# Block-diagonal product of an attention block as two products of 288 columns in one tile of two PSUM banks

## The chip, the core and the metric

The kernel runs on one core of a Trainium2 chip. The metric is the device time of one execution in microseconds; where several runs are shown, their median. TensorE is called PE here (its weight loads PEld), VectorE DVE, ScalarE ACT, GpSimd POOL and SyncE SP, as the profile does.

## What is computed

```python
# q, k, v: batch 8, heads 8, sequence 576, head size 64; float32
kv  = einsum('bhsd,bhse->bhde', k, v)           # 64 x 64 for each head
out = einsum('bhsd,bhde->bhse', q, kv)
rms = sqrt(mean(out * out, axis=-1, keepdims=True) + 1e-06)
x   = out / rms * g_norm                        # -> (4608 tokens, 512)
h   = x @ w_in                                  # 512 -> 2048
sp  = maximum(h, 0) + log1p(exp(-abs(h)))       # softplus
y   = (h * erf(sp)) @ w_out                     # 2048 -> 512
```

## The kernel before

The tokens of one batch entry are worked on as 512 columns (`G`), and the other 64 of each (`R`) are gathered from all eight entries into a ninth step of 512 columns. So `T` counts nine steps: 0 to 7 are the entries, 8 (`B`) the gathered rests. Features lie on partitions, tokens on columns.

**The feed-forward part** fills most of PE's time. From T = 2 (`FIRST`) on, every large product is made from three FP32R products: `product()` (L449) accumulates eight in `n_ps` and four in `m_ps` (L462), and the three forms of each operand are cut by ACT and DVE (`upper`, L405; `lower`, L408 and L411). ACT (L836) and DVE (`add`, L445) join the two sums. Six PSUM banks go round for these products, so a pair of banks comes up again three products later. The hand-written order runs in batches of four blocks of 128 hidden features: four `hidden` products, then four `result` products of the batch before (L847 to L861).

**The attention of entry T + 1** is spread over the batches of entry T, one pair of heads (`p`, 0 to 3) to a batch. `attention()` returns a pair's pieces, and the loop puts them at the places 0, 2, 3, 5, 6 and 8 of a batch (L801):

- `products` (place 0): k^T v of two heads into the diagonal blocks of a bank (L297); in even pairs the transpose of q's last rows for two pairs (L305); DVE's copies of the two blocks into `bd_kv` (L312) and, in even pairs, of the transposed rests into `qT_last` (L315); four transposes of q (L319) and ACT's copy of them into `qT` (L320).
- `apply` (place 2): the product of the rest, 64 columns, into the k-v bank (L324), the product of the 512 columns (L325), DVE's copy of the former into `x_last` (L326), ACT's Square of the latter (L328).
- `halve` (place 3): DVE cuts the squares into an FP32R part and a rest (L338, L339), for T from 2 to 7 (`halves`).
- `mean` (place 5): two FP32R products with a block-diagonal matrix of 1/64 accumulate the mean square (L346, L347); ACT makes the inverse root from it by Ln, Exp and Square (L358 to L360).
- `norm` (place 6): a correction step on DVE (L366, L369) and the scaled output (L378), which reads the L325 bank for the last time.
- `split` (place 8): the three forms of the new x.

For entry 2 the same pieces are laid into the steps of T = 1 (`pieces_of`, L599), and for T = 0 and 1 the mean is one float32 product (L351). All PSUM tiles of a pair come from `ps_at`, a pool of two banks used in turn: k-v products, q's transposes, the 512-column product, the mean. So the next pair's k-v products write the bank that L378 reads last. The framework puts in the waits between engines; the order on each engine is that of the program.

In float32 a product is issued as two PE instructions, in FP32R as one.

Of the kernel before, what the change touches and what calls it, by code (L numbers as in the profile page):

```python
# [39 lines left out]
FP32 = mybir.dt.float32  # L40
# [3 lines left out]
AF = mybir.ActivationFunctionType  # L44
ALU = mybir.AluOpType
PSUM = bass.MemoryType.PSUM
# [8 lines left out]
FIRST = 2  # L55
# [5 lines left out]
def kernel(  # L61
# [10 lines left out]
    nc = tc.nc  # L72
    P = 128
    B, H, S, D = q.shape
    DM, DF = moe_w_in.shape[0], moe_w_in.shape[1] // 2
    J = 4
    G = J * P
    R = S - G
# [8 lines left out]
    attp = ctx.enter_context(tc.tile_pool(name="attp", bufs=1))  # L87
# [5 lines left out]
    first_w = room.enter_context(tc.tile_pool(name="first_w", bufs=1, side="right"))  # L93
    gate = room.enter_context(tc.tile_pool(name="gate", bufs=7, side="right"))
    early = early_room.enter_context(tc.tile_pool(name="early", bufs=2))
    ps_at = ctx.enter_context(tc.tile_pool(name="ps_at", bufs=2, space=PSUM))
    ps_h = ctx.enter_context(tc.tile_pool(name="ps_h", bufs=2, space=PSUM))
    ps_o = ctx.enter_context(tc.tile_pool(name="ps_o", bufs=1, space=PSUM))

    ctx.enter_context(tc.manual_schedule())  # L100

# [51 lines left out]
    for i in range(2):  # L153
        nc.gpsimd.dma_start(
            out=g_col[i * D : i * D + D, :], in_=g_norm.rearrange("(d one) -> d one", one=1)
# [11 lines left out]
    ident = const.tile([P, P], FP32, name="ident")  # L167
    make_identity(nc, ident)
    mean_w = const.tile([P, P], FP32R, name="mean_w")
# [13 lines left out]
    x_last = const.tile([P, KC, G], FP32, name="x_last")  # L183
# [79 lines left out]
    xT, x_forms, tails = {}, {}, {}  # L263
# [5 lines left out]
    def attention(T, p, pools=None):  # L269

        st = {}

        halves = FIRST <= T < B
        bd = bd_kv[:, (T * NP + p) % 2, :]

        q_tail, o_tail = slice(P, 2 * P), slice(2 * P, 2 * P + R)

        def bank(name):
            pool, tag = (pools or {}).get(name, (ps_at, "at"))
            return pool.tile([P, G], FP32, name=name, tag=tag)  # L280

        def square_tile(name):

            if T == 0:
                return gate.tile([P, G], FP32, name=name, tag="h")
            return attp.tile([P, G], FP32, name=name, tag="qT")

        def products():

            kv_ps = st["kv"] = bank("kv_ps")  # L290
            ks, vs, qs = (x.pop((T, p)) for x in (k_sb, v_sb, q_sb))
            C = chunks(T)
            for c in range(C):
                rows = slice(0, S // C + (c < S % C))
                for i in range(2):
                    s = slice(i * D, i * D + D)
                    nc.tensor.matmul(  # L297
                        kv_ps[s, s],
                        lhsT=ks[rows, i, c],
                        rhs=vs[rows, i, c],  # L300
                        start=(c == 0),
                        stop=(c == C - 1),
                    )
            if p % 2 == 0:
                nc.tensor.transpose(kv_ps[:, q_tail], q_last[:, p // 2], ident)  # L305
            if p == NP - 2:
                for i in range(NP):
                    load_last(T + 1, i)
            st["qT"] = square_tile("qT")
            for i in range(2):  # L310
                s = slice(i * D, i * D + D)
                nc.vector.tensor_copy(out=bd[s, s], in_=kv_ps[s, s])  # L312
            if p % 2 == 0:
                tails[T] = attp.tile([P, P], FP32, name="qT_last", tag="t")
                nc.vector.tensor_copy(out=tails[T], in_=kv_ps[:, q_tail])  # L315
            st["tail"] = tails[T][:, p % 2 * R : p % 2 * R + R]
            qt_ps = bank("qt_ps")
            for j in range(J):
                nc.tensor.transpose(qt_ps[:, j * P : j * P + P], qs[:, j], ident)  # L319
            nc.scalar.copy(st["qT"], qt_ps)  # L320

        def apply():
            qT, o_ps, kv_ps = st["qT"], bank("se_ps"), st.pop("kv")
            nc.tensor.matmul(kv_ps[:, o_tail], lhsT=bd, rhs=st.pop("tail"), start=True, stop=True)  # L324
            nc.tensor.matmul(o_ps, lhsT=bd, rhs=qT, start=True, stop=True)  # L325
            nc.vector.tensor_copy(out=x_last[:, p, T * R : T * R + R], in_=kv_ps[:, o_tail])  # L326
            st["o"] = o_ps
            nc.scalar.activation(qT, o_ps, AF.Square)  # L328

        def square():  # L330
            st["o"], st["qT"] = x_last[:, p, :], square_tile("sq")
            nc.scalar.activation(st["qT"], st["o"], AF.Square)

        def halve():
            sq = st.pop("qT")
            hi = st["hi"] = attp.tile([P, G], FP32R, name="sq_hi", tag="rms_r")
            lo = st["lo"] = attp.tile([P, G], FP32R, name="sq_lo", tag="sq_lo")
            nc.vector.tensor_copy(out=hi, in_=sq)  # L338
            nc.vector.tensor_tensor(out=lo, in0=sq, in1=hi.bitcast(FP32), op=ALU.subtract)  # L339

        def mean(table=True):
            ms = st["ms"] = bank("ms_ps")
            if halves:


                nc.tensor.matmul(ms, lhsT=mean_w, rhs=st.pop("hi"), start=True, stop=False)  # L346
                nc.tensor.matmul(ms, lhsT=mean_w, rhs=st.pop("lo"), start=False, stop=True)  # L347
                u = square_tile("u")
            else:
                u = st.pop("qT")  # L350
                nc.tensor.matmul(ms, lhsT=mean_w.bitcast(FP32), rhs=u, start=True, stop=True)  # L351
            if T > 0:
                r = attp.tile([P, G], FP32, name="rms_r", tag="rms_r")
                exp_ln_table()
            else:
                r = gate.tile([P, G], FP32, name="rms_r", tag="s")
            st["u"], st["r"] = u, r
            nc.scalar.activation(r, ms, AF.Ln, bias=eps_col)  # L358
            nc.scalar.activation(r, r, AF.Exp, scale=-0.5)
            nc.scalar.activation(u, r, AF.Square)  # L360
            if table and (T > 0 or p == NP - 1):
                softplus_table()

        def norm():
            ms, u, r = (st.pop(name) for name in ("ms", "u", "r"))
            nc.vector.scalar_tensor_tensor(  # L366
                out=u, in0=ms, scalar=EPS, in1=u, op0=ALU.add, op1=ALU.mult
            )
            nc.vector.scalar_tensor_tensor(  # L369
                out=u, in0=u, scalar=3.0, in1=r, op0=ALU.subtract, op1=ALU.mult  # L370
            )
            if T < FIRST:
                if T not in xT:
                    xT[T] = wide.tile([P, KC, G], FP32, name="xT", tag="ab"[T])
                x = xT[T][:, p, :]
            else:
                x = st["x"] = x_new.tile([P, G], FP32, name="x", tag="x")
            nc.vector.scalar_tensor_tensor(  # L378
                out=x,
                in0=st.pop("o"),  # L380
                scalar=gm_col,
                in1=u,
                op0=ALU.mult,
                op1=ALU.mult,
            )

        def split():
            if T >= FIRST:
                thirds(st.pop("x"), *(form[:, p] for form in x_forms[T]))

        def loads():
            load_pair(T * NP + p + 2)

        if T == 0:
            return products, apply, halve, mean, norm
        if T == B:
            return lambda: None, square, lambda: None, mean, norm, split

        pieces = ((products,), (apply,), (halve, loads)) if halves else ((products, loads), (apply,), ())
        return (*(partial(chain, *group) for group in pieces), mean, norm, split)  # L400


# [111 lines left out]
    o_ps = {}  # L514
# [129 lines left out]
    for n in range(FIRST * FC + 1):  # L644
        T, f = divmod(n, FC)
        if n == FC:
            early_room.close()
            late = ctx.enter_context(tc.tile_pool(name="late", bufs=1))
            x_new = ctx.enter_context(tc.tile_pool(name="x_new", bufs=1))
            acc = ctx.enter_context(tc.tile_pool(name="acc", bufs=1))  # L650
            w_in_p = ctx.enter_context(tc.tile_pool(name="w_in_p", bufs=BATCH))
            low = low_room.enter_context(tc.tile_pool(name="low", bufs=1))
            forms = late.tile([P, 3, KC, G], FP32R, name="x_forms0")
            x_forms[FIRST] = [forms[:, i] for i in range(3)]
# [24 lines left out]
        elif T < FIRST:  # L679
# [10 lines left out]
            for i, c in blocks:  # L690
                nc.tensor.matmul(  # L691
                    plain[i],
                    lhsT=w_in_sb[:, c, i % FC * P : i % FC * P + P],
                    rhs=xT[T][:, c, :],
                    start=(c == 0),
                    stop=(c == KC - 1),
# [89 lines left out]
    for m in range(first_batch, batches + 1):  # L786
        T, b = divmod(m, NB)
# [108 lines left out]
```

## Time and profile before

| | us |
|---|---|
| median of 3 runs | 948.07 (947.21 to 948.4) |
| profiled execution, device time | 947.5 |
| its span in the profile | 945.7 |
| PE, PEld busy | 926.8, 683.3 |
| DVE, ACT busy | 740.5, 615.7 |
| float32 product of 512 columns, L325: 64 instructions | 35.4 |
| float32 product of 64 columns, L324: 64 instructions | 10.9 |
| FP32R products of the mean, L346 and L347: 24 each | 9.5 and 9.5 |

The profile is of one execution, and its span lies 1.8 us below that execution's device time. "Busy" is the union of an engine's instructions; the ends of PE's are modelled, and neighbouring ones overlap, so one instruction's recorded duration is not its price: the step from one end to the next is. The granted clock of PE was 1.0 throughout. The page gives for each group of instructions the line, the engine, the tiles it writes and reads, the count, the busy time, the mean duration and what ended the idle time before it.

### The profile page before, as it was taken

The page shows a single profiled execution, that of the slowest core. Times are in us where ns is not written, and L with a number is a line of the kernel's source. Part 1 is how long each engine was busy: PE and PEld are TensorE (multiplying, and loading weights), DVE is VectorE, ACT ScalarE, POOL GpSimd, SP SyncE. Part 2 cuts the span into 40 slices and gives each one's busy share as a digit, 9 for nine tenths or more (in the row PEclk, how much of TensorE's full clock was granted, in tenths as well). Part 3 has the DMA queues.
Part 4 walks back from the last instruction along what each step waited for, and adds up shares of the span by engine and source line. Part 5 has one row for each costly group of instructions (what it writes and reads, how often), then busy time and mean ns, then how long its engine had stood idle before and what let it go on. Part 6 is the DMA issues. An engine that isn't in the chain of part 4 may idle for free.

```text
span 945.7 us, 11743 instructions
## 1 busy us (share of the span) xinstructions
PE 926.8 (98%) x4272; PEld 683.3 (72%) x4272; DVE 740.5 (78%) x1054; ACT 615.7 (65%) x825; POOL 2.4 (0%) x10
## 2 busy tenths in 40 slices
PE   6999999999999999999999999999999999999998
PEld 4444445665688888888888888888888888878886
DVE  3979958888578788777788888878887877777667
ACT  3889876777666666666666666666666666665552
POOL 1000000000000000000000000000000000000000
PEclk9999999999999999999999999999999999999999
DMA  9856505899699998998899889998896778768872
GB/s 258 282 158 215 169 9 215 310 339 340 219 364 346 317 303 284 315 301 303 275 295 314 303 288 311 312 301 294 293 323 261 265 247 352 284 245 309 335 273 60
DMA packets 111842, 259.78 MB, mean 275 GB/s; under 512 B 43864, under 2 KB 69544, under 8 KB 111784
## 3 DMA queue, kind: packets, MB, share of 16 engines
q1 hardware_dynamic: 110152, 256.73, 78.4%
q10 hardware_dynamic: 1568, 2.29, 0.8%
q8 instruction: 34, 0.56, 0.2%
q14 instruction: 24, 0.20, 0.1%
q0 software_dynamic: 64, 0.00, 0.0%
HBM read 224.40 MB, written 34.60 MB: 274 GB/s over the span
## 4 chain that ended last, share of the span: by engine, by line
PE 88%; ACT 5%; DVE 5%; DMA 1%; issue 1%; DVEq 0%
PE n_ps L462 45%; PE m_ps L462 23%; PE o_ps L520 8%; PE h_ps L691 3%; PE se_ps L325 3%; PE kv_ps L297 2%; PE qt_ps L319 2%; ACT w_e L215 1%; ACT w_m L219 1%; DMA q_sb<-in_q_dram 1%; PE ms_ps L347 1%; PE ms_ps L346 1%; PE ms_ps L351 1%; ACT L103 1%; ACT s_sb L719 1%
## 5 line engine op out<-in xcount | busy, mean ns | idle before, releaser
L462 PE MATMUL n_ps<-x_forms,w_in_parts 128*128 128x512 f32 x896 | 233.2, 402 | 1.6 <-DVE x_forms L408 0.7
L462 PE MATMUL n_ps<-w_out_parts,g_forms 128*128 128x512 f32 x928 | 231.2, 391 | 0.0
L462 PEld LDWEIGHTS n_ps<-w_out_parts,g_forms 128*128 128x128 f32 x928 | 174.2, 188 | 38.4 <-issue 1.7
L462 PEld LDWEIGHTS n_ps<-x_forms,w_in_parts 128*128 128x128 f32 x896 | 166.7, 188 | 45.3 <-issue 9.1
L838 ACT ACTIVATE s<-h 128x512 f32<-128x512 f32 x112 | 71.0, 634 | 180.4 <-DVE h L445 180.4
L445 DVE TENSOR_TENSOR h<-m_ps,h 128x512 f32<-128x512 f32 x116 | 79.8, 688 | 60.9 <-ACT h L836 41.5
L462 PE MATMUL m_ps<-w_out_parts,g_forms 128*128 128x512 f32 x464 | 124.2, 389 | 0.0
L462 PE MATMUL m_ps<-x_forms,w_in_parts 128*128 128x512 f32 x448 | 120.0, 390 | 0.0
L520 PE MATMUL o_ps<-w_out_sb,h_sb 128*128 128x512 f32 x224 | 100.8, 593 | 0.3 <-DVE h_sb L642 0.3
L462 PEld LDWEIGHTS m_ps<-w_out_parts,g_forms 128*128 128x128 f32 x464 | 87.1, 188 | 18.1
L462 PEld LDWEIGHTS m_ps<-x_forms,w_in_parts 128*128 128x128 f32 x448 | 84.1, 188 | 17.7
L445 DVE TENSOR_TENSOR e<-m_ps,e 128x512 f32<-128x512 f32 x116 | 80.3, 692 | 18.3 <-PE m_ps L462 11.2
L440 DVE SCALAR_TENSOR_TENSOR e<-n_ps,e 128x512 f32<-128x512 f32 x88 | 60.3, 686 | 39.6 <-PE n_ps L462 39.6
L520 PEld LDWEIGHTS o_ps<-w_out_sb,h_sb 128*128 128x128 f32 x224 | 42.3, 190 | 48.9 <-issue 46.6
L411 DVE SCALAR_TENSOR_TENSOR g_forms<-g_forms 128x1024 fp32r<-128x1024 f32 x58 | 71.1, 1225 | 2.0
L408 DVE TENSOR_TENSOR g_forms<-h,g_forms 128x1024 fp32r<-128x1024 f32 x58 | 70.6, 1218 | 1.7 <-ACT g_forms L405 1.4
L836 ACT ACTIVATE h<-n_ps 128x512 f32<-128x512 f32 x112 | 65.5, 585 | 3.9 <-PE n_ps L462 3.8
L405 ACT ACTIVATE g_forms<-h 128x1024 fp32r<-128x1024 f32 x58 | 58.8, 1058 | 12.4 <-PE m_ps L462 9.8
L856 DVE TENSOR_TENSOR h<-h,s 128x1024 f32<-128x1024 f32 x56 | 66.0, 1218 | 0.7 <-ACT s L842 0.7
L691 PE MATMUL h_ps<-xT,w_in_sb 128*128 128x512 f32 x144 | 64.9, 594 | 0.8 <-DVE w_in_sb L240 0.6
L106 ACT ACT_TABLE_LOAD x44 | 56.5, 1283 | 0.7
L842 ACT ACTIVATE s<-s 128x1024 f32<-128x1024 f32 x56 | 56.3, 1053 | 0.3
(98 smaller groups left out, 1014.3 us busy)
## 6 DMA issues: line engine op xcount, KB each, us to landing
w_out_parts<-w_out SPq DMA_DIRECT2D x116, 768.0 KB
w_in_parts<-w_in SPq DMA_DIRECT2D x112, 768.0 KB
w_in<-w_new SPq DMA_DIRECT2D x16, 768.0 KB
q_sb<-in_q_dram SPq DMA_DIRECT2D x32, 256.0 KB
w_raw<-in_moe_w_out_dram SPq DMA_DIRECT2D x8, 1024.0 KB
out_dram<-e SPq DMA_DIRECT2D x32, 256.0 KB
k_sb<-in_k_dram SPq DMA_DIRECT2D x28, 287.5 KB
v_sb<-in_v_dram SPq DMA_DIRECT2D x28, 287.5 KB
```

Of the source, the lines that this page charges most:

```text
L106: nc.scalar.preload_act_table_set("softplus")
L405: nc.scalar.activation(high, x, AF.Copy, scale=1.0 + 2.0**-13)
L408: nc.vector.tensor_tensor(out=low, in0=x, in1=high.bitcast(FP32), op=ALU.subtract)
L411: nc.vector.scalar_tensor_tensor(out=both, in0=low.bitcast(FP32), scalar=SHIFT, in1=high.bitcast(FP32), op0=ALU.mult, op1=ALU.add,)
L440: nc.vector.scalar_tensor_tensor(out=out_, in0=ps, scalar=scale, in1=out_, op0=ALU.mult, op1=ALU.add)
L445: nc.vector.tensor_tensor(out=out_, in0=ps, in1=out_, op=ALU.add)
L462: nc.tensor.matmul(ps, lhsT=weights(form, k), rhs=moving(form, k), start=(form == forms[0] and k == 0), stop=(form == forms[-1] and k == 3),)
L520: nc.tensor.matmul(o_ps[j], lhsT=g[:, j * P : j * P + P], rhs=w_out_sb[:, f, :], start=(f == 0), stop=last,)
L691: nc.tensor.matmul(plain[i], lhsT=w_in_sb[:, c, i % FC * P : i % FC * P + P], rhs=xT[T][:, c, :], start=(c == 0), stop=(c == KC - 1),)
L836: nc.scalar.activation(h[:, i], n_ps, AF.Copy, scale=SHIFT - 1.0)
L838: nc.scalar.activation(s[:, i], h[:, i], AF.Softplus)
L856: nc.vector.tensor_tensor(out=part(h, half), in0=part(h, half), in1=part(s, half), op=ALU.mult)
```

## The change

For T = 2 and later a pair gets one tile of two banks, `two_banks()`, from a new pool `ps_two` with one buffer, instead of tiles from the two buffers of `ps_at`, whose banks are freed when T = 1 begins. The k-v products and the mean of T = 8 take its first bank, q's transposes its second.

For T from 2 to 7, `qT` becomes two halves of 288 columns: 256 of the 512, and 32 of the pair's 64 rest columns behind them. The product is two products of 288 columns, one into each bank, in place of one of 64 and one of 512. The mean becomes two accumulations of 256 columns, each into the other half of a bank. `qT_last` of 128 columns is gone there: the rest is copied into `qT`, for the even pair from PSUM, for the odd one from a small tile kept for it. Square, the cutting and the norm run over 2 x 256 columns.

The four transposes of q stand ahead of the four loads of `q_last` and of DVE's copies out of the tile, in all steps.

```diff
         def bank(name):
+            if T >= FIRST:
+                return two_banks()[:, name in ("qt_ps", "se_ps")]
             pool, tag = (pools or {}).get(name, (ps_at, "at"))
             return pool.tile([P, G], FP32, name=name, tag=tag)
 
-        def square_tile(name):
+        def two_banks():
+            if "two" not in st:
+                st["two"] = ps_two.tile([P, 2, G], FP32, name="at_ps", tag="at")
+            return st["two"]
+        HG, HR = G // 2, R // 2
+        def twofold(x):
+            return x.rearrange("p (i n) -> p i n", i=2) if halves else x
+        def square_tile(name, tail=False):
 
             if T == 0:
                 return gate.tile([P, G], FP32, name=name, tag="h")
-            return attp.tile([P, G], FP32, name=name, tag="qT")
+            t = attp.tile([P, 2, HG + HR], FP32, name=name, tag="qT")
+            if tail:
+                return t
+            return t[:, :, :HG] if halves else t.rearrange("p i n -> p (i n)")[:, :G]
...
                 nc.tensor.transpose(kv_ps[:, q_tail], q_last[:, p // 2], ident)
+            qt_ps = bank("qt_ps")
+            for j in range(J):
+                nc.tensor.transpose(qt_ps[:, j * P : j * P + P], qs[:, j], ident)
             if p == NP - 2:
                 for i in range(NP):
                     load_last(T + 1, i)
-            st["qT"] = square_tile("qT")
+            st["qT"] = square_tile("qT", halves)
             for i in range(2):
                 s = slice(i * D, i * D + D)
                 nc.vector.tensor_copy(out=bd[s, s], in_=kv_ps[s, s])
-            if p % 2 == 0:
-                tails[T] = attp.tile([P, P], FP32, name="qT_last", tag="t")
-                nc.vector.tensor_copy(out=tails[T], in_=kv_ps[:, q_tail])
-            st["tail"] = tails[T][:, p % 2 * R : p % 2 * R + R]
-            qt_ps = bank("qt_ps")
-            for j in range(J):
-                nc.tensor.transpose(qt_ps[:, j * P : j * P + P], qs[:, j], ident)
-            nc.scalar.copy(st["qT"], qt_ps)
+            if halves:
+                tail = tails.pop(T) if p % 2 else kv_ps[:, P : P + R]
+                nc.vector.tensor_copy(out=st["qT"][:, :, HG:], in_=twofold(tail))
+                if p % 2 == 0:
+                    tails[T] = attp.tile([P, R], FP32, name="qT_next", tag="t")
+                    nc.vector.tensor_copy(out=tails[T], in_=kv_ps[:, P + R : 2 * P])
...
+            if halves:
+                nc.scalar.copy(st["qT"][:, :, :HG], twofold(qt_ps))
+            else:
+                nc.scalar.copy(st["qT"], qt_ps)
 
         def apply():
+            if halves:
+                qT, two = st.pop("qT"), two_banks()
+                del st["kv"]
+                for i in range(2):
+                    nc.tensor.matmul(
+                        two[:, i, : HG + HR], lhsT=bd, rhs=qT[:, i], start=True, stop=True
+                    )
+                nc.vector.tensor_copy(
+                    out=twofold(x_last[:, p, T * R : T * R + R]), in_=two[:, :, HG : HG + HR]
+                )
+                o_ps = st["o"] = two[:, :, :HG]
+                qT = st["qT"] = qT[:, :, :HG]
+                nc.scalar.activation(qT, o_ps, AF.Square)
+                return
...
         def mean(table=True):
-            ms = st["ms"] = bank("ms_ps")
+            ms = st["ms"] = two_banks()[:, :, HG:] if halves else bank("ms_ps")
             if halves:
-                nc.tensor.matmul(ms, lhsT=mean_w, rhs=st.pop("hi"), start=True, stop=False)
-                nc.tensor.matmul(ms, lhsT=mean_w, rhs=st.pop("lo"), start=False, stop=True)
+                hi, lo = (twofold(st.pop(name)) for name in ("hi", "lo"))
+                for i in range(2):
+                    nc.tensor.matmul(ms[:, i], lhsT=mean_w, rhs=hi[:, i], start=True, stop=False)
+                    nc.tensor.matmul(ms[:, i], lhsT=mean_w, rhs=lo[:, i], start=False, stop=True)
...
         if n == FC:
             early_room.close()
+            at_room.close()
+            ps_two = ctx.enter_context(tc.tile_pool(name="ps_two", bufs=1, space=PSUM))
```

The operations of `halve` and `norm` keep their number and their elements; their access patterns become 2 x 256.

More of the change, by code (lines that the diff above doesn't have):

```diff
@@ L95 @@
     early = early_room.enter_context(tc.tile_pool(name="early", bufs=2))
-    ps_at = ctx.enter_context(tc.tile_pool(name="ps_at", bufs=2, space=PSUM))
     ps_h = ctx.enter_context(tc.tile_pool(name="ps_h", bufs=2, space=PSUM))
     ps_o = ctx.enter_context(tc.tile_pool(name="ps_o", bufs=1, space=PSUM))
+    at_room = ctx.enter_context(ExitStack())
+    ps_at = at_room.enter_context(tc.tile_pool(name="ps_at", bufs=2, space=PSUM))
     ctx.enter_context(tc.manual_schedule())
@@ L312, in products @@
                 nc.vector.tensor_copy(out=bd[s, s], in_=kv_ps[s, s])
-            if p % 2 == 0:
-                tails[T] = attp.tile([P, P], FP32, name="qT_last", tag="t")
-                nc.vector.tensor_copy(out=tails[T], in_=kv_ps[:, q_tail])
-            st["tail"] = tails[T][:, p % 2 * R : p % 2 * R + R]
-            qt_ps = bank("qt_ps")
-            for j in range(J):
-                nc.tensor.transpose(qt_ps[:, j * P : j * P + P], qs[:, j], ident)
-            nc.scalar.copy(st["qT"], qt_ps)
-        def apply():
+            if halves:
[5 more added lines that the diff above has]
+            else:
+                if p % 2 == 0:
+                    tails[T] = early.tile([P, P], FP32, name="qT_last", tag="t", bufs=1)
+                    nc.vector.tensor_copy(out=tails[T], in_=kv_ps[:, q_tail])
+                st["tail"] = tails[T][:, p % 2 * R : p % 2 * R + R]
+            if halves:
+                nc.scalar.copy(st["qT"][:, :, :HG], twofold(qt_ps))
+            else:
+                nc.scalar.copy(st["qT"], qt_ps)
+        def apply():
+            if halves:
[12 more added lines that the diff above has]
+                return
             qT, o_ps, kv_ps = st["qT"], bank("se_ps"), st.pop("kv")
@@ L337, in halve @@
             lo = st["lo"] = attp.tile([P, G], FP32R, name="sq_lo", tag="sq_lo")
-            nc.vector.tensor_copy(out=hi, in_=sq)
-            nc.vector.tensor_tensor(out=lo, in0=sq, in1=hi.bitcast(FP32), op=ALU.subtract)
+            nc.vector.tensor_copy(out=twofold(hi), in_=sq)
+            nc.vector.tensor_tensor(
+                out=twofold(lo), in0=sq, in1=twofold(hi.bitcast(FP32)), op=ALU.subtract
+            )
         def mean(table=True):
-            ms = st["ms"] = bank("ms_ps")
+            ms = st["ms"] = two_banks()[:, :, HG:] if halves else bank("ms_ps")
             if halves:
-                nc.tensor.matmul(ms, lhsT=mean_w, rhs=st.pop("hi"), start=True, stop=False)
-                nc.tensor.matmul(ms, lhsT=mean_w, rhs=st.pop("lo"), start=False, stop=True)
+                hi, lo = (twofold(st.pop(name)) for name in ("hi", "lo"))
+                for i in range(2):
+                    nc.tensor.matmul(ms[:, i], lhsT=mean_w, rhs=hi[:, i], start=True, stop=False)
+                    nc.tensor.matmul(ms[:, i], lhsT=mean_w, rhs=lo[:, i], start=False, stop=True)
                 u = square_tile("u")
@@ L352, in mean @@
             if T > 0:
-                r = attp.tile([P, G], FP32, name="rms_r", tag="rms_r")
+                r = twofold(attp.tile([P, G], FP32, name="rms_r", tag="rms_r"))
                 exp_ln_table()
@@ L378, in norm @@
             nc.vector.scalar_tensor_tensor(
-                out=x,
+                out=twofold(x),
                 in0=st.pop("o"),
```

## The prediction

> **What bounds the kernel now.** I read the busy shares first, then the chain that ended last, then the stretches of the span, and last the single products that the change replaces.
>
> ```profile
> span 945.7 us, 11743 instructions
> ...
> PE 926.8 (98%) x4272; PEld 683.3 (72%) x4272; DVE 740.5 (78%) x1054; ACT 615.7 (65%) x825; POOL 2.4 (0%) x10
> ...
> PE 88%; ACT 5%; DVE 5%; DMA 1%; issue 1%; DVEq 0%
> ```
>
> PE is busy nearly all the time and carries 88% of the chain. The table by stretch (span in us, length, then PE, PEld, DVE and ACT busy, then clock and DMA share) says where:
>
> ```profile
> 250.00:500.00 250.00, 249.69 (x1266) 200.21 (x1265) 198.80 (x285) 163.94 (x218) 0.00 (x0) 1.00 0.89 303
> 500.00:745.00 245.00, 245.00 (x1255) 198.00 (x1254) 197.26 (x283) 156.31 (x207) 0.00 (x0) 1.00 0.88 302
> ```
>
> In the stretch that holds the attention of batch entries 3 to 7, PE never rests, at full clock, while DVE has a fifth of the time free and ACT a third. So time taken off PE there comes off the end, and time added to DVE or ACT costs only where PE waits for it. The change acts on 24 head pairs (entries 2 to 7, four each). Entry 2's four lie between 145 and 250 us, where PE is busy 100 of 100 us too.
>
> The chain in order of time (start, us, work, instructions) prices the products. A float32 product is two PE instructions, an FP32R product one.
>
> ```profile
> 205.35 0.17 PE kv_ps L324 x2
> 205.52 0.91 PE se_ps L325 x2
> 206.43 3.43 PE o_ps L520 x8
> ...
> 509.21 0.17 PE kv_ps L324 x2
> 509.38 0.91 PE se_ps L325 x2
> ...
> 518.49 0.23 PE ms_ps L346
> 518.72 0.23 PE ms_ps L347
> 518.95 1.83 PE n_ps L462 x8
> ```
>
> To be seen: 0.17 us for the tail product of 64 columns, 0.91 for the product of 512, 0.23 for each FP32R product of the mean. L520 has 512 float32 columns as well, and one instruction of it takes 3.43 / 8 = 0.429. So L325, at 2 x 0.429 = 0.858, pays 0.055 too much, and L324, at 64/512 of that = 0.107, pays 0.06 too much. The weight loads (start, us) say why:
>
> ```profile
> 509.05 0.19 PEld L324 LDWEIGHTS kv_ps<-qT_last,bd_kv 128*128 128x128 f32 x1
> 509.16 0.30 PEld L325 LDWEIGHTS se_ps<-qT,bd_kv 128*128 128x128 f32 x2
> ```
>
> Loads follow each other at 0.11 us (509.05 to 509.16; and 0.30 less one load's 0.19). A 64-column instruction streams for 0.054 and then waits for the next load: one such wait inside L324, one ahead of L325.
>
> **What the Trainium skill says.** "TensorE: Matmul & The Clock Gate", Back-to-back issue gap, gives N/2.4 + 2.5 ns a pass. The trace agrees for float32 if a column takes two cycles: 2 x 512/2.4 + 2.5 = 429. FP32R stands at 227 to 236 ns instead of 216, so 11 to 20 ns are unexplained. The same page, LDWEIGHTS, gives columns/1.2 = 107 ns, against 110 measured. "PSUM — Partial Sum Buffer", PSUM bank collisions, says that two engines may not be on one bank and quadrant at once, reads included, so such pairs must be ordered; the trace fits: the copies at L312 were released by the transpose at L305, which writes other columns of the same bank. "VectorE: DVE Perf Modes", Mode 2×_2P, asks for SBUF operands that split in half along the outer dimension: L338 takes 419 ns where L339 takes 692, and 2 x 256 still splits in half.
>
> **The change part by part.**
>
> 1. *Block-diagonal product.* Removed: 2 x 64 and 2 x 512 columns, 0.17 + 0.91 = 1.081 us (read from the single instructions; 1.081 or 1.082 in all 24). Added: four instructions of 288 columns, 2 x 288/2.4 + 2.5 = 242 ns each, 0.970 together. The column count is the same; each load (0.11) now lies under 0.24 of streaming. Gain 0.111 a pair, 2.66 us for 24, all on PE. Bounds: if the float32 rate holds, 0.10 to 0.12; I see no mechanism for a loss.
>
> 2. *Mean.* Removed: two FP32R instructions of 512, 0.464. Added: four of 256, a form that the trace doesn't have. Lower bound: the load pitch, 4 x 0.11 = 0.44. Proportional to columns: 0.464. With the whole excess over 213 ns (14 ns) paid per instruction: 4 x 0.121 = 0.484. Upper bound: a half-width product as slow as a full one, 4 x 0.231 = 0.92, if the load's own 188 ns plus the 39 ns that lie between a load's end and the next start were what sets 227. Against this: behind the transposes, loads for L462 start at 503.45 and 503.56, so the first was in use 0.11 later. I take +0.015 a pair, 0.36 us in all; the ends are -0.6 and +11.
>
> 3. *PE order.* q's transposes were already next in PE's queue behind L297 and L305; only their place ahead of DVE's copies in the program changes. Nothing. The four q_last loads are issued behind them in the program, but SP runs them in its own order and they wait for L305 alone; if they took the transposes along, 0.6 us on data needed a whole entry later. Nothing.
>
> 4. *DVE.* Even pairs: L315 (0.29) becomes two copies of 64 columns, about 0.21 each as L326; odd pairs get one more. So +0.13 to +0.21 us in 24.8 us, of which DVE is idle 4.8. The wait added: the product needs the tail copy. Before, the bd copies end 2.5 to 2.6 us ahead of it for entries 3 to 7 (506.45 against 509.05); entry 2's second pair has 0.51. Nothing; 0.2 once if that pair is late.
>
> 5. *One bank shared by two readers.* ACT's Square (L328) and DVE's copy to x_last (L326) now read the same two banks, so Square waits for the copy. Queued behind Square on ACT is the next L836, and behind that DVE's L445. But for entries 3 to 7 the copy already ends first:
>
> ```profile
> 512.66 0.21 DVE L326 COPY x_last<-kv_ps 128x64 f32<-128x64 f32 x1
> ...
> 513.31 0.58 ACT L328 ACTIVATE qT<-se_ps 128x512 f32<-128x512 f32 x1
> ```
>
> 0.44 us to spare. In entry 2 Square starts ahead of the copy's end in all four pairs, by 1.04, 0.16, 0.13 and 0.16: about 1.5 us of ACT's time where ACT is 72% busy. Bound on PE: 0 to 0.5 us once.
>
> 6. *One tile for all of a pair.* The next pair's k-v products wait for the last reader, L378, as they do now; the margin there is the thinnest of all:
>
> ```profile
> 501.21 0.75 DVE L378 SCALAR_TENSOR_TENSOR x<-se_ps,gm_col,u 128x512 f32<-128x512 f32 x1
> ...
> 502.22 0.20 PEld L297 LDWEIGHTS kv_ps<-v_sb,k_sb 116*64 116x64 f32 x4 [0.35 <-DVE x L378]
> ```
>
> From L378's end to L297 are 0.258 us; where PE really waits for DVE, it starts 0.054 behind it. PE's own step from L462 into L297 is 318 ns, in the one case with 0.177 as well, so L378 isn't what it waits for, and some 0.2 is left. L378's end hangs on PE through L445, L856, L366 and L369, so it keeps its distance. L366 and L378 get strided PSUM operands: 2 x 256 instead of 512. The strided 4 x 256 of L856 costs no more than its elements (1218 for 1024, 684 for 512), so I take 0; bound, 0.1 each before PE loses anything.
>
> Sum: -2.66 + 0.36 = **-2.3 us**. Against the profiled execution (947.5 us, of which 945.7 are span): span 943.4, execution 945.2. The median of the runs shown, 948.07, lies 0.57 above that execution; less 2.3 it gives **945.8**.
>
> **The rivals.**
>
> *A: as summed, 945.8* (945.0 to 946.4 with the mean between proportional and +0.03 and entry 2 losing up to 0.3).
>
> *B: gain and loss meet, 946.2 to 949.* The three strided operations of the norm run 0.1 longer each; the margin of 0.2 goes, and 20 pairs wait 0.1: +2 us, 947.8. Or, the two banks being one tile, ACT's copy of qT waits for DVE's copies of k-v: ACT starts it at 503.76, DVE ends about 506.9, so ACT stands for 3.1 us and L405 and L836 behind it too. PE next needs qT at 509.05, and the n_ps bank that L836 frees had 3.6 us to spare at least; so the gain would mostly survive. For it: nothing shows whether waits go by bank or by tile.
>
> *C: slower.* The half-width FP32R product isn't cheaper than the full one. It decides from 0.144 us an instruction ((0.464 + 0.111)/4, the gain is gone); slower by 0.2% from 0.163; at the full 0.231 it is +11.0 - 2.7 = +8.4, 956.5. For it: FP32R's unexplained excess and 188 + 39 = 227. Against: the load taken up after 0.11.
>
> *D: the change is not effective*, because something else holds the pace. PE's full stretches speak against it; DMA's share of 0.89 is the nearest; if it were the pace, 948.
>
> **How the numbers follow.** A measurement of this kernel can tell about 0.2% (1.9 us) from no change: faster is below 946.17, slower above 949.97. A 0.56, B and D 0.22, C and other losses 0.22. A ends almost wholly in faster (0.54), B and D mostly within: faster 0.55, same 0.24, slower 0.21. The likeliest case spans 945.0 to 946.4; to hold 8 in 10 the range must take in B, D and the first part of C: 945.0 to 951.0.
>
> **What would show it.** Right: the product's four instructions at 0.24 in the chain, 0.97 a pair; the mean's four at 0.12, 0.46 to 0.49; no wait of PE ahead of the k-v products; a batch (one pair each) at 24.62 and 24.74 us in turn instead of 24.72 and 24.84. Wrong: 0.2 each in the mean (C); PE or PEld waiting at the k-v products or the product itself (B).

## The result and the profile after

The changed kernel takes 976.06 us in the median of four runs (975.53 to 977.92), the kernel before 947.81 in the same comparison: 3.0% slower, ratio 1.0302 with a 95% interval of 1.0284 to 1.0319. The forecast was 945.8, with a range up to 951.0.

The page of the changed kernel, its span, its engines and its chain:

```profile
span 976.1 us, 11965 instructions
...
PE 928.8 (95%) x4320; PEld 691.4 (71%) x4320; DVE 743.9 (76%) x1078; ACT 616.3 (63%) x825; POOL 2.4 (0%) x10
...
PE 84%; ACT 6%; DVE 5%; issue 3%; DMA 1%; SPq 0%; DVEq 0%
```

PE's busy time has hardly changed (926.8 to 928.8), and the span has grown by 30.4. (2.2 us of that lie ahead of the changed part: entry 2's first k-v product starts at 146.98 us instead of 144.82. This execution, 977.92 us, was the longest of the four.) So PE works no longer, it waits. The table by stretch says where (length, then PE, PEld, DVE, ACT busy):

```profile
250.00:500.00 250.00, 237.98 (x1228) 192.45 (x1227) 190.94 (x281) 153.38 (x204) 0.00 (x0) 1.00 0.84 288
500.00:745.00 245.00, 231.77 (x1199) 190.12 (x1198) 188.21 (x277) 147.47 (x197) 0.00 (x0) 1.00 0.85 291
```

PE, without a gap here before, now lacks 12.0 and 13.2 us. Of its waits (total us, times, longest) one is new and large:

```profile
PE at_ps L316 <- issue: 26.5, 18, 1.6
```

L316 is the k-v product (L297 before). "issue" means that the profile names no releaser. The chain of one batch shows the rest:

```profile
524.61 0.97 PE at_ps L357 x4
...
533.80 0.12 PE at_ps L394
533.92 0.12 PE at_ps L395
534.04 0.12 PE at_ps L394
534.16 0.12 PE at_ps L395
...
542.48 1.53 issue
544.01 0.80 PE at_ps L316 x20
```

Both new products cost what was forecast, 0.97 and 0.48 us. Then PE stands for 1.53 us. From one k-v product to the next it takes 26.14 and 26.39 us in turn instead of 24.72 and 24.84: 1.5 us more in each of 18 batches. Behind the last pair PE waits once more for the norm: the waits of L510 (L462 before) for `x_forms` are 2.9 us in all and were 1.4. The 18 batches bring 26.7 us and this wait 1.5, together the 28 of the result.

What L316 waits for is seen in order of time (start, us, engine, line; in brackets the idle time before and its releaser):

```profile
514.65 0.63 ACT L408 ACTIVATE u<-rms_r 128x512 f32<-128x512 f32 x1
...
515.32 0.69 DVE L414 SCALAR_TENSOR_TENSOR u<-at_ps,u 128x512 f32<-128x512 f32 x1 [1.55 <-ACT u L408]
516.04 0.69 DVE L417 SCALAR_TENSOR_TENSOR u<-u,rms_r 128x512 f32<-128x512 f32 x1
516.77 0.75 DVE L426 SCALAR_TENSOR_TENSOR x<-at_ps,gm_col,u 128x512 f32<-128x512 f32 x1
...
517.59 0.23 PEld L316 LDWEIGHTS at_ps<-v_sb,k_sb 116*64 116x64 f32 x4 [1.80 <-issue]
```

The loads of L316 start 0.07 us behind the end of L426 (L378 before), the tile's last reader, and so in all 18 batches with this wait; from this step, and not from a releaser that the profile names, I read what they wait for. The norm's three operations last as long as before (0.69, 0.69, 0.75), but start late: DVE waited 1.55 us for ACT's L408. DVE's wait for that operation was 4.2 us in two places before and is 34.7 in 21 now. And ACT is late from the first thing that it does in the batch:

```profile
522.01 0.22 DVE L338 COPY qT<-at_ps 128x64 f32<-128x64 f32 x1
522.15 0.21 DVE L341 COPY qT_next<-at_ps 128x64 f32<-128x64 f32 x1
522.46 0.59 ACT L348 COPY qT<-at_ps 128x512 f32<-128x512 f32 x1 [4.27 <-DVE qT_next L341]
```

ACT's copy of q's transposes, which lie in the second bank, starts when DVE's copies out of the first bank are done. The transposes had ended at 519.12, so ACT stood 3.34 us for nothing. In odd pairs the releaser is another line, as ACT's waits for the whole kernel show (total us, times, longest):

```profile
ACT qT L348 <- DVE qT_next L341: 43.3, 12, 4.3
ACT qT L348 <- DVE bd_kv L335: 41.0, 11, 3.9
```

Before, the copy waited for PE alone:

```profile
ACT qT L320 <- PE qt_ps L319: 33.9, 24, 7.8
```

The line with L335 settles what the wait is about. In odd pairs DVE also writes into `qT` (L338, from an SBUF tile), after L335; but ACT is let go by L335, which touches only `bd_kv` and the tile's first bank. So the wait is between two reads of one PSUM tile, in different banks. The new order alone doesn't do it: in entries 0 and 1 the changed kernel has the same order but separate tiles, and there ACT's copy goes ahead of DVE's where it can (at 69.62 us, DVE's first copy at 71.10).

### The profile page after: what moved, and what is told of

Same layout as the page of the kernel before. It is cut to its first block, busy times and chain, and to the rows that moved or that the text cites. A ratio compares the mean times of both kernels' runs of the same rounds, so it can differ in the third digit from the quotient of the medians.

```text
span 976.1 us, 11965 instructions
## 1 busy us (share of the span) xinstructions
PE 928.8 (95%) x4320; PEld 691.4 (71%) x4320; DVE 743.9 (76%) x1078; ACT 616.3 (63%) x825; POOL 2.4 (0%) x10
## 4 chain that ended last, share of the span: by engine, by line
PE 84%; ACT 6%; DVE 5%; issue 3%; DMA 1%; SPq 0%; DVEq 0%
PE n_ps L510 43%; PE m_ps L510 22%; PE o_ps L568 8%; PE h_ps L741 3%; PE at_ps L357 2%; PE at_ps L316 2%; PE at_ps L328 1%; DMA v_sb<-in_v_dram 1%; ACT w_e L217 1%; ACT L105 1%; DMA q_last<-in_q_dram 1%; ACT w_m L221 1%; DVE h L493 1%; PE at_ps L395 1%; PE at_ps L394 1%
## 5 line engine op out<-in xcount | busy, mean ns | idle before, releaser
L510 PE MATMUL n_ps<-x_forms,w_in_parts 128*128 128x512 f32 x896 | 230.1, 398 | 2.9 <-DVE x_forms L456 1.6
L510 PE MATMUL n_ps<-w_out_parts,g_forms 128*128 128x512 f32 x928 | 231.3, 391 | 0.0
L510 PEld LDWEIGHTS n_ps<-w_out_parts,g_forms 128*128 128x128 f32 x928 | 173.0, 188 | 36.7 <-issue 1.7
L510 PEld LDWEIGHTS n_ps<-x_forms,w_in_parts 128*128 128x128 f32 x896 | 166.7, 188 | 39.7 <-DVE x_forms L456 2.2
L888 ACT ACTIVATE s<-h 128x512 f32<-128x512 f32 x112 | 71.0, 634 | 155.2 <-DVE h L493 155.2
L493 DVE TENSOR_TENSOR h<-m_ps,h 128x512 f32<-128x512 f32 x116 | 79.8, 688 | 59.6 <-ACT h L886 41.5
L510 PE MATMUL m_ps<-w_out_parts,g_forms 128*128 128x512 f32 x464 | 124.2, 389 | 0.0
L510 PE MATMUL m_ps<-x_forms,w_in_parts 128*128 128x512 f32 x448 | 120.2, 390 | 0.0
L510 PEld LDWEIGHTS m_ps<-w_out_parts,g_forms 128*128 128x128 f32 x464 | 87.1, 188 | 18.1
L510 PEld LDWEIGHTS m_ps<-x_forms,w_in_parts 128*128 128x128 f32 x448 | 84.1, 188 | 18.1
L493 DVE TENSOR_TENSOR e<-m_ps,e 128x512 f32<-128x512 f32 x116 | 80.3, 692 | 16.0 <-PE m_ps L510 6.9
L348 ACT COPY qT<-at_ps 128x512 f32<-128x512 f32 x24 | 14.1, 586 | 84.3 <-DVE qT_next L341 43.3
```

The lines of the kernel that those rows point to most:

```text
L493: nc.vector.tensor_tensor(out=out_, in0=ps, in1=out_, op=ALU.add)
L510: nc.tensor.matmul(ps, lhsT=weights(form, k), rhs=moving(form, k), start=(form == forms[0] and k == 0), stop=(form == forms[-1] and k == 3),)
L888: nc.scalar.activation(s[:, i], h[:, i], AF.Softplus)
```

## The experiments

**Theory:** ACT's copy is held for DVE's last read anywhere in the tile; the lateness runs down ACT's queue to the norm, and so to the next pair's k-v products. **Rivals:** the one buffer alone does it; or the halves do.

**ACT's copy first.** In the changed kernel:

```diff
             st["qT"] = square_tile("qT", halves)
+            if halves:
+                nc.scalar.copy(st["qT"][:, :, :HG], twofold(qt_ps))
             for i in range(2):
...
-            if halves:
-                nc.scalar.copy(st["qT"][:, :, :HG], twofold(qt_ps))
-            else:
+            if not halves:
                 nc.scalar.copy(st["qT"], qt_ps)
```

> The changed kernel with one line moved: ACT's copy of q's transposes is issued ahead of DVE's copies out of the same two-bank tile. Theory (ACT's copy is held for the last DVE read of the tile, ACT then runs 3.1 to 3.3 us late, the norm ends late and the next pair's k-v products wait): ACT starts within 0.1 us of the transposes' end, DVE's copies come later anyway and lose nothing, PE no longer waits, and the gain of the products is left: 945.2 to 946.4 us. Rival (the wait comes from the one buffer, the k-v products waiting for the last reader of the whole tile, whatever ACT does): no change, 974 to 978 us.

Measured: 947.02 us (946.36 to 947.92 over 21 runs), against 948.06 before; ratio 0.9988, interval 0.9982 to 0.9995. The wait is gone:

```profile
503.80 0.59 ACT L334 COPY qT<-at_ps 128x512 f32<-128x512 f32 x1 [1.13 <-PE at_ps L328]
...
506.04 0.45 DVE L337 COPY bd_kv<-at_ps 64x64 f32<-64x64 f32 x2
```

ACT is released by PE's transposes again, and DVE reaches its own copies two microseconds later anyway. One line's place is worth 29 us. The rival falls: with ACT on time PE waits nowhere for the single buffer. But the time stays 0.6 above the expected range; this is taken up below.

**The tile alone, both orders.** The kernel before gets the two-bank tile and the early transposes; its products and its mean stay. ACT's copy stands behind DVE's copies in the first kernel and ahead of them in the second. Of the diff, the part that makes the tile:

```diff
         def bank(name):
+            if T >= FIRST:
+                if "two" not in st:
+                    st["two"] = ps_two.tile([P, 2, G], FP32, name="at_ps", tag="at")
+                return st["two"][:, name in ("qt_ps", "se_ps")]
```

> The kernel before with the shared two-bank tile and the transposes ahead alone: the products stay one of 64 and one of 512 columns, the mean two of 512. Theory (the tile's wait is the whole loss): the changed kernel's time plus the products' gain of 2.2 us, 976 to 981 us, with ACT's copy held 3 us by DVE. Rival (the halves, their strided operands or four products in the mean make the loss): 947 to 949 us.

> As the kernel before with the shared tile and the transposes ahead, and ACT's copy ahead of DVE's copies. Theory: nothing left to wait for and no gain, 947 to 949 us; set beside the same order with the halves it gives the products' gain by itself, 2.0 to 2.7 us. Rival (one buffer): 974 to 981 us.

Measured: 975.42 us with ACT behind (ratio 1.0290, 1.0276 to 1.0304), 948.12 with ACT first (0.9998, 0.9990 to 1.0006). ACT waits in the first as in the changed kernel:

```profile
ACT qT L325 <- DVE qT_last L323: 42.7, 12, 4.2
ACT qT L325 <- DVE bd_kv L320: 41.0, 11, 3.9
```

So the whole loss comes with the tile and the order; the halves have no part in it that these runs could tell. I had expected the first to lie 2.2 us above the changed kernel; it doesn't (975.42 and 976.06). Where PE waits for the norm anyway, a shorter product only makes the wait longer: PE waits 26.5 us at the k-v products of the changed kernel and 24.7 here. With ACT first in both, the kernel with the halves is 1.1 us faster (947.02 and 948.12), where I had expected 2.0 to 2.7; that is taken up with the prediction's sum.

**The transposes behind DVE's copies.** The changed kernel with the four transposes moved back down, ahead of ACT's copy.

> The changed kernel with q's transposes put back behind DVE's copies in the program. Theory (waits go by the whole tile, also for PE writing one bank while DVE reads the other): PE stands at the transposes until DVE's copies end, 3.3 to 3.8 us in each of some 20 pairs, while ACT is then late by no more than PE: 1005 to 1030 us. Rival (only reads by two engines are ordered across the tile, PE's writes by bank): PE goes on, 974 to 978 us as the changed kernel.

Measured: 1064.15 us (ratio 1.1226, 1.1182 to 1.1269).

```profile
PE at_ps L346 <- DVE bd_kv L332: 38.0, 12, 3.5
PE at_ps L346 <- DVE qT_next L338: 36.1, 12, 3.6
```

PE stands at the transposes for DVE's reads of the other bank, 74 us in all: a PE write waits across the tile as well. The time went past my range by a second effect, seen in the chain:

```profile
506.79 1.11 PE at_ps L346 x4
507.90 3.41 PE n_ps L510 x8
511.31 1.16 PE m_ps L510 x4
512.47 1.81 PE n_ps L510 x8
```

After such a wait eight products take 3.41 us instead of 1.85, and the transposes and the next four are slow too: up to 2.5 us more in a pair. The profiled execution (1068.3 us) lost 121 us against the one of the kernel before, 47 of them beside the waits, which is 2.5 in each of the 19 pairs with the longest waits. The table by stretch has the granted clock as the third number from the end; it is 0.50 while these eight products run:

```profile
507.90:511.30 3.40, 3.40 (x9) 2.63 (x9) 1.76 (x2) 2.49 (x3) 0.00 (x0) 0.50 0.00 0
```

The mean of the whole span fell to 0.94. The Trainium skill, "TensorE: Matmul & The Clock Gate", What's actually happening, says that the clock halves once PE has been idle for a window of about 3.4 us. The trace agrees: around the end of each of the 19 waits of 3.5 and 3.6 us the clock was halved, around one of 2.07 it wasn't. But it was around one of 2.75 too, so 3.4 us of waiting is no sharp limit here. So the early transposes are what keeps this tile from costing 12%; ACT's copy needed the same.

**ACT late by a set amount.** To price the lateness by itself, the kernel before, with its own tiles, copies q's transposes three, five and six times over in three kernels. The diff is the first's.

```diff
-            nc.scalar.copy(st["qT"], qt_ps)
+            for _ in range(3 if T >= FIRST else 1):
+                nc.scalar.copy(st["qT"], qt_ps)
```

> The kernel before, unchanged but that ACT copies q's transposes three times over instead of once (for entries 2 to 7), so ACT is about 1.1 us late in each pair, with no shared tile and no wait. Theory (PE loses what ACT's lateness has over a slack; the changed kernel was late by 3.2 us a pair and its batch grew by 1.5, so the slack is about 1.65): no loss, 947 to 949.5 us. Rival (ACT's lateness goes into the pace one for one): about +1 us a pair, 968 to 974. Rival (ACT's lateness costs nothing, the tile does): 947 to 949.

> As the last, with five copies instead of one: ACT about 2.1 us late. Theory (slack 1.65): 0.45 a pair over 20 pairs, 953 to 961 us. One for one: 988 to 998. Lateness costs nothing: 947 to 949.

> With six copies: ACT about 2.65 us late. Theory: 1.0 a pair, 963 to 972 us. One for one: 999 to 1009. Lateness costs nothing: 947 to 949.

Measured: 948.18 us (ratio 1.0003, 0.9995 to 1.0012), 950.58 (1.0028, 1.0017 to 1.0038) and 964.07 (1.0168, 1.0154 to 1.0182). Repeated copies follow each other at 0.62 us, more than I had put in, so ACT was 1.24, 2.48 and 3.10 us late. In the steady batches (entries 3 to 7) that cost 0.00, 0.02 and 0.58 us each. So there is a slack, a lateness that costs nothing, but it is about 2.5 us and not 1.65. The second kernel lies below its range for that reason; the third lies inside its own by luck, for a batch grew by 0.58 instead of 1.0, and entry 2, which I had left out, added 3.5 us. And 3.1 us of lateness cost a batch 0.58 us here, where the changed kernel lost 1.49 with 3.2. Something else took 0.85 us of slack. The chain of the last of the three tells what:

```profile
509.29 0.64 ACT u L361
...
509.96 0.70 DVE u L367
510.66 0.02 issue
510.68 0.70 DVE u L370
511.39 0.02 issue
511.41 0.76 DVE x L379
512.17 0.04 issue
512.22 0.66 PE qt_ps L319 x4
```

With the old tiles it is not the k-v products but q's transposes that wait for the norm's last operation (L379). The k-v products take the mean's bank, which the first norm operation (L367) frees; here they start 0.6 us before the last one does:

```profile
510.80 0.66 PEld L297 LDWEIGHTS kv_ps<-v_sb,k_sb 116*64 116x64 f32 x20 [0.35 <-DVE u L367]
```

In the shared tile they wait for the last one, and come before the transposes: 0.73 us (odd pairs) to 0.99 us (even) earlier.

**The same lateness in the shared tile.** The kernel with the tile, the old products and ACT's copy first, and more copies of `qT` onto itself on ACT, which touch no PSUM: five in the first kernel, whose diff is shown, four in the second.

```diff
             nc.scalar.copy(st["qT"], qt_ps)
+            for _ in range(5 if T >= FIRST else 0):
+                nc.scalar.copy(st["qT"], st["qT"])
```

> The kernel with the shared tile and ACT's copy first (products as before), with five more copies of qT onto itself on ACT, so ACT is about 3.1 us late as in the run with six copies, but now one tile holds all of a pair. In the kernel before, the k-v products wait for the first norm operation on DVE, which frees the mean's bank, and only q's transposes, 0.7 to 1.0 us later, for the last; in one tile the k-v products wait for the last. Theory (this takes 0.85 us of the slack, 2.5 before, 1.65 now): 1.45 us a pair, 972 to 980 us. Rival (ACT's lateness alone counts, whatever frees the tile): 962 to 966 us as without the tile.

> As the last with four more copies, ACT about 2.5 us late. Theory: 0.8 us a pair, 960 to 968 us. Rival: 949.5 to 952 us as without the tile.

Measured: 985.37 us (ratio 1.0399, 1.0383 to 1.0414) and 969.63 (1.0233, 1.0216 to 1.0250). The copies onto itself follow each other at 0.65 us, so ACT was a little later than I had put in. In the steady batches, with the lateness of ACT's copy over that in the kernel before:

| kernel | ACT late by | growth of a batch | slack: the difference |
|---|---|---|---|
| own tiles, three copies | 1.24 us | 0.00 | at least 1.24 |
| own tiles, five copies | 2.48 | 0.02 | 2.46 |
| own tiles, six copies | 3.10 | 0.58 | 2.52 |
| shared tile, four more copies | 2.61 | 0.93 | 1.68 |
| shared tile, five more copies | 3.26 | 1.58 | 1.68 |
| shared tile alone, ACT behind | 3.14 | 1.45 | 1.68 |
| changed kernel | 3.17 | 1.49 | 1.68 |

The tile's later release takes some 0.85 us of slack, as the theory had it. Both totals lie above my ranges, by 2 to 5 us: ACT was 0.1 to 0.2 us later in each batch than I had put in, and the extra copies also fell on entry 2's four pairs, which I had left out. From its first k-v product to entry 3's it takes 113.83 and 112.31 us, against 110.19 with the tile and ACT first alone. The wait is the one of the changed kernel:

```profile
495.46 1.44 issue
496.90 0.80 PE at_ps L302 x20
```

So the loss has two parts that act together. With ACT on time the release costs nothing (948.12); with the old tiles lateness of 3.1 costs 16 us, 3.5 of them in entry 2; both together cost 28.

Where the slack lies can be read by setting the changed kernel's trace beside the one before, each batch from its first k-v product on. ACT's copy ends 3.0 and 3.3 us later in turn, L408 (L360 before) only 1.8 and 2.0: ACT takes up about 1.3 us in waits of its own (those for L445, L493 now, shrink from 180.4 us in all to 155.2). Some 0.25 lie between the end of L360 and the start of L366, and 0.16 between the norm and the k-v products. That makes the 1.7; the old order of release adds the 0.85.

**The order by entry.** With ACT first, entry 2 lost: from its first k-v product to entry 3's it took 110.40 us against 109.58 before. There DVE is free when the products end, and its copies had to wait for ACT's. So ACT's copy goes first for entries 3 to 7 and stays behind in entry 2:

```diff
             st["qT"] = square_tile("qT", halves)
-            if halves:
+            if halves and T > FIRST:
                 nc.scalar.copy(st["qT"][:, :, :HG], twofold(qt_ps))
...
+            if halves and T == FIRST:
+                nc.scalar.copy(st["qT"][:, :, :HG], twofold(qt_ps))
```

> The changed kernel with ACT's copy first for entries 3 to 7 and DVE's copies first for entry 2, where DVE is free when the k-v products end. Theory (ACT first cost entry 2 about 0.7 us there, because DVE's copies waited for ACT and the cut squares came late to the mean): 0.5 to 0.9 us below the kernel with ACT first throughout, 946.0 to 946.6. Rival (entry 2's loss comes from the shared tile whichever engine is first): as that kernel, 946.8 to 947.4.

Measured: 946.55 us against 947.85 before (ratio 0.9984, 0.9978 to 0.9991), the fastest of all the kernels run. In the trace entry 2 takes 109.64 us, 0.76 less than with ACT first throughout, as expected. In the runs the two kernels, compared with the kernel before, differ by 0.26 us only, and their intervals overlap: the better total is likely, not shown.

## Why the prediction was wrong

*What bounds the kernel* was right: PE without a gap, and time taken off it comes off the end.

*Step 1, the product:* right to the nanosecond, 0.970 us (four at 242 to 243 ns).

*Step 2, the mean:* right, 0.481 us where 0.479 was taken. Rival C is out: a half-width FP32R product takes 120 ns.

*The sum of the two* was 0.096 us a pair; with ACT first a batch got shorter by 0.07 (24.65 and 24.77). The products themselves gave 0.094. The FP32R products around them took some 27 ns more per batch in sum, a few tenths of a nanosecond each. Why is open. This, and entry 2's loss, put the time with ACT first above its range.

*Step 3, the transposes' place:* nothing was lost by it, but it is no matter of indifference: without it 12%. I had reasoned that PE's own order stays the same, and not asked what PE waits for.

*Step 4, DVE's copies:* right in size (0.22, 0.21, 0.20 us) and that the product doesn't wait for them. That ACT's copy might wait for them I put under rival B. The first cut of the squares takes 419 ns over 2 x 256 columns too, as had been taken (L382, L338 before).

*Step 5, the two readers in `apply`:* right for entries 3 to 7, where nothing waits there; in entry 2 ACT waited 2.0 us in four places, where I had put 1.5.

*Step 6 failed, in two places.* "As they do now" was wrong: before, the k-v products waited for the first norm operation, and the transposes for the last. The sentence on the kernel before which says that the k-v products write the bank that L378 reads last is wrong in the same way. The trace's release by L378 0.26 us ahead of L297 was a coincidence of time. And "so it keeps its distance": I followed L378's end back to PE through L856 and left out ACT's L360, which ended at 499.51, 0.26 us ahead of L366's start. That margin was in the trace, and it is a part of the slack of 1.7 us. In place of a norm that keeps its distance, the runs showed one that comes some 1.6 us late in each batch, and PE waiting 1.5 us for it in 18 of them.

*Rival B* named the mechanism and its size, ACT standing 3.1 us (3.1 to 3.3 measured). Its price failed: I looked for what needs `qT` and the n_ps bank, found both with time to spare, and wrote that the gain would mostly survive. ACT's lateness wasn't followed to the end of its queue, through the Erf and the table load to L358, L360 and the norm. 3.1 less the slack of 1.68 that the runs then showed for this tile is 1.4 us a batch, some 27 us for 19. With the queue followed, case B's range would have reached to about 976, and with it mine.

## What to carry to other kernels

When an edit joins banks in one tile, list every pair of engines that touches any part of it, reads too, and issue them in the order in which the engines get there: one line's place was worth 29 us here, and by the traces the right place differed between entries (entry 2 took 109.64 us with ACT behind, 110.40 with ACT first). Follow the lateness of an engine down its own queue to the next thing that the bound engine waits for, and not only to the next reader of the delayed data. And ask of each joined buffer which operation freed it before, and which frees it now.

## What the runs showed of the hardware

A float32 product of 288 columns takes 242 to 243 ns an instruction and one of 512 takes 429. From the two, a column costs 0.83 ns, and 2 to 3 ns are fixed. An FP32R product takes 227 ns at 512 columns and 120 at 256: 0.42 ns a column, and about 13 fixed. A wait of PE of 3.5 us cost up to 2.5 us more in the products behind it, which ran at a granted clock of 0.50.
